# Whole comparisons instead of halves in the routing that runs beside the experts

## The chip, the cores and the metric

The kernel runs on one core of one Trainium2 chip. The metric is the device time of one execution, in microseconds (us); less is better. The engines have short names in the profile: PE is TensorE (matrix products), PEld its weight loads, DVE is VectorE, ACT is ScalarE, POOL is GpSimd, SP is SyncE, which issues DMAs here.

## The reference

Attention over 8 batches, 8 heads, 576 positions of 64 values, in two parts that are added: attention over queries, keys and values averaged in groups of four, repeated four times, and local attention in which each position sees those less than 4 away. The result is seen as 4608 tokens of 512 values. Then a mixture of 8 experts:

```python
logits = x @ w_gate                       # 4608 x 8
order = np.argsort(-logits.flatten())
for idx in order:                         # best pairs (token, expert) first
    tok, e = idx // E, idx % E
    if assigned[tok] >= 0 or counts[e] >= cap: continue   # cap = 4608 / 8 = 576
    assigned[tok] = e; counts[e] += 1
for e in range(E):
    h = np.maximum(x[assigned == e] @ w1[e], 0.0)         # 512 -> 1024
    out[assigned == e] = h @ w2[e]                        # 1024 -> 512
```

Every expert ends with exactly 576 tokens, but which ones follows from a greedy pass over all 36864 logits in order of size.

## The kernel before, in words

**Attention** (the first 290 us) writes the tokens to a table in DRAM and leaves the logits in SBUF: 128 partitions x 36 columns of tokens (`NT` = 36) x 8 experts. Its instructions stand in an order written out by hand.

**Routing** (`Routing`) does not sort. It goes in eight phases, each of which finds the expert that fills up next, the limit in logit value at which it does, and so its list of 576 tokens (`idx`). The best logit of each open token is made an integer key of two 16-bit halves, `xh` and `xl`, each copied 16 wide. To find a limit, `count` compares the key with a set of thresholds, counts per expert how many tokens reach each, and narrows down in three levels: 64 thresholds (`cmp0`, made by `first_compare`), then 32, then 32 (`cmp32`). It is called twice a phase, for the high and the low half. A comparison is a VectorE instruction over (tokens, thresholds) that gives ones and zeros; the counting is a group of TensorE products of these with the marks of each token's best expert (`oh`, `ol`), into a PSUM tile `pR`: 18 products for 64 thresholds, 9 for 32. Small steps follow: `cs`, a product with an identity (line 735), `fl`, a product with ones (line 740), `nj`, and the next thresholds `thr`. Each waits for the one before.

`emit` turns the marks of the chosen tokens into the list. It ranks them, splits the rank into a high and a low part, and makes two one-hot tables, `ohh` (18 wide) and `ohl` (32 wide, line 985); 18 products of `ohl` with `r` (made of `ohh`) give `idx`. The last phase has nothing to search and runs `emit` alone.

Each of these comparisons is cut in parts along the columns of tokens, so that TensorE can start on the first part while VectorE compares the second: `HALF` gives the cuts of `cmp0` and `cmp32` (0 to 20 and 20 to 36), and `EH` those of `ohl` (0 to 18 and 18 to 36).

```python
HALF = {16: ((0, NT),), 32: ((0, 20), (20, NT)), 64: ((0, 20), (20, NT)), 128: ((0, 12), (12, 24), (24, NT))}
EH = ((0, 18), (18, NT))
```

**Experts** (`Experts`): for each, `gather` fetches its rows of the token table into `xg` with GpSimd's indirect DMAs, five pieces (line 1061). ScalarE and VectorE split them into two float16 parts `xs` (lines 1080 and 1081), and DMA transposes issued by SP make `xt` from these. `mlp` multiplies with the first weights into `pH` (line 1097), ScalarE and VectorE make the two parts of `ht` (lines 1110 and 1113), and the second products go into `pX` (line 1126), from where ScalarE and VectorE make `y` (1131 and 1133), which GpSimd scatters to the output (1134). Weights come in as float32 and are split into `wh` (ScalarE, 1044) and `wl` (VectorE, 1046).

**Order.** The first phase runs alone after attention, since the first expert needs its list; the later seven are written ahead of the expert before theirs, with a high priority, so they run beside its products:

```python
for i in range(E):
    if more:
        with tc.high_priority():
            idx2, raw = ro.phase(i + 2 == E, False, ...)
        ...
    ex.mlp(w, xt, idx, in1, in2)
```

From the end of attention on, a planner fixes the order of each engine's instructions before the run, from modelled durations, dependences and priorities. On the chip each engine takes its instructions in that order, and a waiting one holds up those behind it.

Of the kernel before, what the change touches and what calls it, by code (L numbers as in the profile page):

```python
# [30 lines left out]
NT = NTOK // 128  # L31
# [590 lines left out]
CAP = NTOK // E  # L622
LV = ((64, 1024), (32, 32), (32, 1))
SW = 16
HALF = {16: ((0, NT),), 32: ((0, 20), (20, NT)), 64: ((0, 20), (20, NT)), 128: ((0, 12), (12, 24), (24, NT))}
XSB = 2
LOE = "vector"
RACT = True
EH = ((0, 18), (18, NT))
# [15 lines left out]
class Routing:  # L645
# [51 lines left out]
    def compare(self, cmp, key, thr, a, b):  # L697
        w = min(SW, thr.shape[1])
        r = thr.shape[1] // w
        self.nc.vector.tensor_tensor(cmp[:, a:b].rearrange("p t (r j) -> p t r j", r=r),  # L700
                                     key[:, a:b, None, :w].to_broadcast([128, b - a, r, w]),
                                     thr.rearrange("p (r j) -> p r j", r=r)[:, None].to_broadcast([128, b - a, r, w]),
                                     op=OP.is_ge)
# [7 lines left out]
    def count(self, oh, key, cmp, cap):  # L711


        nc, wk = self.nc, self.wk
        base = self.base
        for lv, (J, step) in enumerate(LV):
            if lv:
                cmp = wk.tile([128, NT, J], BF, name=f"cmp{J}")
                for a, b in HALF[J]:
                    self.compare(cmp, key, thr, a, b)  # L720
            n = 128 // J if J < 64 or lv == 0 else 1
            cnt = self.ps.tile([128, 8 * E], F32, name="pR", bufs=2)[:, :n * E]
            cv = cnt.rearrange("p (e i) -> p e i", e=E)
            for t in range(0, NT, n):
                m = min(n, NT - t)
                nc.tensor.matmul(cv[:m * J, :, :m], cmp[:, t:t + m].rearrange("p t j -> p (t j)"), oh[:, :, t:t + m],  # L726
                                 start=t == 0, stop=t + m == NT, skip_group_check=True)
            if n > 1:


                cs = wk.tile([128, 8 * E], F16, name="cs")
                nc.vector.tensor_scalar(cs[:, :n * E], cnt, 2000.0, None, op0=OP.min)
                cnt = self.ps.tile([128, E], F32, name="pR", bufs=2)
                for i in range(n):
                    nc.tensor.matmul(cnt[:J], self.id16[:, J * i:J * i + J], cs[:, i:n * E:n], start=i == 0,
                                     stop=i == n - 1)
            fl = wk.tile([128, E], BF, name="fl")
            nc.vector.tensor_tensor(fl[:J], cnt[:J], cap()[:J], op=OP.is_ge)
            njp = self.ps.tile([128, E], F32, name="pR", bufs=2)
            nc.tensor.matmul(njp, self.one[:J], fl[:J], start=True, stop=True)  # L740
            nj = wk.tile([128, 1], F32, name="nj", bufs=2)
            nc.vector.tensor_reduce(nj, njp, axis=AX.X, op=OP.max)
            if lv < 2:
                w, n = LV[lv + 1][0], base.shape[1]
                thr = wk.tile([128, w], I16, name=f"thr{w}", bufs=2)
                nc.vector.scalar_tensor_tensor(thr, nj.to_broadcast([128, w]), float(step), base[:, :w],
                                               op0=OP.mult, op1=OP.add)
                rest = wk.tile([128, 65], F32, name="rest", bufs=2)[:, :n - w]
                nc.vector.scalar_tensor_tensor(rest, nj.to_broadcast([128, n - w]), float(step), base[:, w:],
                                               op0=OP.mult, op1=OP.add)  # L750
                base = rest
        v = wk.tile([128, 1], F32, name="val", bufs=2)
        nc.vector.tensor_tensor(v, nj, base, op=OP.add)
        return v
# [27 lines left out]
    def setup(self, a, b, first=False):  # L782
# [7 lines left out]
        def t(name, dt=F32, shape=(128, NT), keep=True, mid=False):  # L790
            if not keep:
                return su.tile(list(shape), dt, name=name)[..., a:b]
            if name not in self.v:
                self.v[name] = su.tile(list(shape), dt, name=name)
            return self.v[name][:, a:b] if mid else self.v[name][..., a:b]
# [11 lines left out]
        def spread(x, k):  # L807
            o = t(x, I16, (128, NT, SW), True, True)
            for c in range(0, n, 18):
                d = min(n, c + 18)  # L810
                i = k[:, c:d, None].to_broadcast([128, d - c, SW])
                if first and b < NT and x in SPP:
                    nc.gpsimd.tensor_copy(o[:, c:d], i)
                else:
                    nc.scalar.copy(o[:, c:d], i)
                yield
# [39 lines left out]
    def phase(self, last, first=False, known=None):  # L856
# [4 lines left out]
        def t(name, dt=BF, shape=(128, NT)):  # L861
            return wk.tile(list(shape), dt, name=name)
# [13 lines left out]
        if first:  # L876
            xh = self.v["xh"]
            early = self.first_compare(xh, self.cuts)
# [3 lines left out]
                pass  # L882
        kh, kl, am, amu, oh, xh, xl = [self.v[n] for n in "kh kl am amu oh xh xl".split()]

        if not first:
            early = self.first_compare(xh, HALF[LV[0][0]])
        H = self.count(oh, xh, early, lambda: self.cap)
        cmp0 = self.first_compare(xl, HALF[LV[0][0]])
        e, g = t("e"), t("g")
        nc.vector.tensor_scalar(e, kh, H, None, op0=OP.is_equal)  # L890
        ol = t("ol", BF, (128, E, NT))
# [64 lines left out]
    def emit(self, f, off, first=False, left=None):  # L956


        nc, wk = self.nc, self.wk
        rk = self.rank(f, left)  # L960
        v0, v1 = wk.tile([128, NT], F32, name="v0"), wk.tile([128, NT], F32, name="v1")
        o8 = wk.tile([128, 1], F32, name="o8")
        nc.vector.tensor_scalar(o8, off, -8192.0, None, op0=OP.add)
        nc.vector.scalar_tensor_tensor(v1, rk[:, 1], o8, f[:, 1], op0=OP.add, op1=OP.mult)
        nc.vector.scalar_tensor_tensor(v0, rk[:, 0], -8192.0, f[:, 0], op0=OP.add, op1=OP.mult)
        pi = wk.tile([128, NT], I32, name="pi")
        nc.vector.scalar_tensor_tensor(pi, v0, 8192.0, v1, op0=OP.add, op1=OP.add)
        ph, pl = wk.tile([128, NT], I32, name="ph"), wk.tile([128, NT], I32, name="pl")
        nc.vector.tensor_scalar(ph, pi, 5, None, op0=OP.arith_shift_right)
        nc.vector.tensor_scalar(pl, pi, 31, None, op0=OP.bitwise_and)  # L970
        ph, pl = ph.bitcast(I16)[:, ::2], pl.bitcast(I16)[:, ::2]
        ohh = wk.tile([128, NT, 18], BF, name="ohh")
        nc.vector.tensor_tensor(ohh, ph[:, :, None].to_broadcast([128, NT, 18]),
                                self.io[:, None, :18].to_broadcast([128, NT, 18]), op=OP.is_equal)
        r = wk.tile([128, NT, 2, 18], BF, name="r")
        nc.vector.tensor_tensor(r[:, :, 0], ohh, self.t128, op=OP.mult)
        if first and RACT:
            nc.scalar.activation(r[:, :, 1], ohh, AF.Copy, scale=self.pcol)
        else:
            nc.vector.tensor_scalar(r[:, :, 1], ohh, self.pcol, None, op0=OP.mult)  # L980
        ohl = wk.tile([128, NT, 32], BF, name="ohl")

        p = self.ps.tile([64, 72], F32, name="pR", bufs=2)
        for a, b in EH:
            nc.vector.tensor_tensor(ohl[:, a:b], pl[:, a:b, None].to_broadcast([128, b - a, 32]),
                                    self.io[:, None, :].to_broadcast([128, b - a, 32]), op=OP.is_equal)
            for t in range(a, b, 2):
                nc.tensor.matmul(p, ohl[:, t:t + 2].rearrange("p t i -> p (t i)"),
                                 r[:, t:t + 2].rearrange("p t s i -> p (t s i)"), start=t == 0, stop=t == NT - 2)
        odd = wk.tile([32, 36], F32, name="odd")  # L990
        nc.vector.tensor_copy(odd, p[32:, 36:])
        sm = wk.tile([32, 2, 18], F32, name="sm")
        nc.vector.tensor_tensor(sm.rearrange("p s i -> p (s i)"), p[:32, :36], odd, op=OP.add)
        idx = self.ix.tile([128, 5], I32, name="idx")
        for g in range(4):
            n = (21 - g) // 4
            self.done = nc.vector.tensor_tensor(idx[32 * g:32 * g + 32, :n], sm[:, 0, g::4], sm[:, 1, g::4], op=OP.add)  # L997
        return idx, rk
# [269 lines left out]
```

## Time and profile before

| what | value |
|---|---|
| median of 3 runs | 799.38 us (798.59 to 804.76) |
| the profiled execution | 796.83 us |
| its span, first to last instruction | 795.0 us |
| PE busy | 684.7 us (86%) |
| DVE busy | 562.3 us (71%), 1679 instructions |
| ACT / POOL busy | 333.4 us / 235.1 us |
| attention | 0 to about 294 us |
| first routing, alone | to about 326 us |
| routing beside experts | about 341 to 622 us |
| experts with no routing beside them | about 622 to 795 us |

The page gives busy time per engine, waits with the instruction that ended them, and the clock that TensorE was granted as a share of full speed. In a list in order of time each row has a start, a length, engine, line, operation and shapes; "x9" means that nine like instructions are merged in the row, and a bracket at the end gives the idle time before it and what ended it. Lengths of neighbours may overlap, since the next instruction starts before the last has fully ended; so starts tell the pace, not lengths.

### The profile page before, as it was taken

To read this page: it belongs to the slowest core of one execution; us is meant where nothing else is said; L and a number is where in the kernel's file an instruction comes from. 1 tells how busy PE (TensorE), PEld (TensorE's weight loads), DVE (VectorE), ACT (ScalarE), POOL (GpSimd) and SP (SyncE) were. 2 spreads that over 40 slices of the span, in tenths; PEclk is the share of its full clock that TensorE was granted. 3 is DMA by queue.
4 is the path that set the end of the run, shared out by engine and by line. 5 is a ranking of instruction groups with operands and counts; after the bars stand their busy time and mean duration, and the time that the engine had idled before them with its cause. 6 is when DMAs were issued, how large, how long until landed. Compare 5 with 4: busy or idle time off the path is not lost.

```text
span 795.0 us, 21152 instructions
## 1 busy us (share of the span) xinstructions
PE 684.7 (86%) x8545; PEld 472.8 (59%) x8545; DVE 562.3 (71%) x1679; ACT 333.4 (42%) x631; POOL 235.1 (30%) x274
## 2 busy tenths in 40 slices
PE   6687988796988873499889899999999979999994
PEld 4576877685877752365456356456456456574752
DVE  6878877977797887887869889888869335172210
ACT  3456756573767440342525234234324134252210
POOL 9264463735355440300400412130220311301001
PEclk8789998998999995599989999999999999999997
DMA  9949979697999850611825744480946832704001
GB/s 265 210 129 238 244 195 268 183 255 204 254 228 211 201 173 9 207 66 59 274 60 212 139 151 162 85 307 2 245 147 233 177 113 94 166 1 100 21 28 34
DMA packets 152901, 126.18 MB, mean 159 GB/s; under 512 B 96996, under 2 KB 127204, under 8 KB 152804
## 3 DMA queue, kind: packets, MB, share of 16 engines
q1 hardware_dynamic: 145424, 103.30, 49.9%
q0 software_dynamic: 6432, 20.98, 8.7%
q8 instruction: 68, 1.11, 0.6%
q10 hardware_dynamic: 948, 0.55, 0.3%
q14 instruction: 29, 0.24, 0.1%
HBM read 95.30 MB, written 21.23 MB: 147 GB/s over the span
## 4 chain that ended last, share of the span: by engine, by line
issue 30%; PE 25%; DVE 20%; DMA 13%; ACT 5%; POOL 4%; SPq 2%; POOLq 0%; ACTq 0%; DVEq 0%
PE pH L1097 7%; PE pX L1126 3%; DMA xt<-xs 3%; POOL out_dram L1134 3%; DMA nat<-in_v_dram 2%; DVE cmp L700 2%; PE g L476 2%; PE g L436 2%; PE g L292 2%; DMA xg<-x_dram,idx 2%; PE pR L726 1%; DMA up_dram<-xu 1%; DVE x L407 1%; PE g L454 1%; PE g L325 1%
## 5 line engine op out<-in xcount | busy, mean ns | idle before, releaser
L1097 PE MATMUL pH<-xt,wh 128*128 128x256 f16 (+1 forms) x1024 | 200.1, 291 | 5.7 <-DMA xt<-xs 5.0
L1126 PE MATMUL pX<-wh,ht 128*128 128x512 f16 (+1 forms) x640 | 183.3, 384 | 0.2 <-ACT y L1131 0.2
L1097 PE MATMUL pH<-xt,wl 128*128 128x320 f16 (+1 forms) x512 | 148.5, 290 | 0.0
L1126 PEld LDWEIGHTS <-ht 128*128 128x128 f16 (+1 forms) x960 | 81.5, 101 | 89.2 <-issue 6.4
L1134 POOL DMA_INDIRECT out_dram<-y,idx x40 | 41.2, 1031 | 289.5 <-ACT y L1131 262.9
L1126 PE MATMUL pX<-wl,ht 128*128 128x512 f16 (+1 forms) x320 | 119.3, 384 | 0.0
L1097 PEld LDWEIGHTS <-wh 128*128 128x128 f16 x1024 | 98.2, 99 | 33.2 <-issue 9.1
L1110 ACT ACTIVATE ht<-pH 128x512 f16<-128x512 f32 (+1 forms) x128 | 45.5, 407 | 128.3 <-PE pH L1097 128.3
L1046 DVE SCALAR_TENSOR_TENSOR wl<-nat,wh 128x512 f16<-128x512 f32 x128 | 85.2, 682 | 2.5
L1113 DVE SCALAR_TENSOR_TENSOR ht<-pH,ht 128x512 f16<-128x512 f32 (+1 forms) x128 | 52.4, 450 | 38.7 <-ACT ht L1110 38.3
L1061 POOL DMA_INDIRECT xg<-x_dram,idx x40 | 43.3, 1083 | 118.2 <-DVE idx L997 57.1
L1131 ACT ACTIVATE y<-pX 128x512 f32<-128x512 f32 (+1 forms) x40 | 23.6, 593 | 117.7 <-PE pX L1126 76.4
L1044 ACT ACTIVATE wh<-nat 128x1024 f16<-128x1024 f32 x64 | 66.8, 1055 | 6.6 <-DMA nat<-in_moe_w_dram 6.5
L1081 DVE SCALAR_TENSOR_TENSOR xs<-xg,xs 128x512 f16<-128x512 f32 (+1 forms) x35 | 23.5, 687 | 50.3 <-ACT xs L1080 50.1
L1097 PEld LDWEIGHTS <-wl 128*128 128x128 f16 x512 | 50.6, 99 | 13.0 <-issue 0.4
L465 ACT COPY pt<-g 64x512 f32<-64x512 f32 x72 | 41.8, 580 | 34.2 <-PE g L454 33.0
L292 PE MATMUL g<-ident,nat 128*128 128x128 f32 x256 | 41.7, 292 | 13.7 <-DMA nat<-in_q_dram 9.5
L476 PE MATMUL g<-vw,pt 128*64 128x65 f32 x1152 | 44.5, 230 | 2.4 <-DMA up_dram<-xu 1.4
L476 PEld LDWEIGHTS g<-vw,pt 128*64 128x64 f32 x1152 | 39.5, 143 | 8.4 <-ACT pt L465 4.5
L278 ACT COPY kt<-g 64x512 f32<-64x512 f32 (+1 forms) x56 | 35.1, 627 | 20.7 <-PE g L292 13.8
L278 ACT COPY qz<-g 64x512 f32<-64x512 f32 (+1 forms) x52 | 33.0, 634 | 21.4 <-PE g L292 19.1
L265 POOL TENSOR_TENSOR gtmp<-qz 64x576 f32<-64x576 f32 x28 | 32.5, 1160 | 30.7 <-DVE kdt L268 29.1
(219 smaller groups left out, 1180.1 us busy)
## 6 DMA issues: line engine op xcount, KB each, us to landing
nat<-in_moe_w_dram SPq DMA_DIRECT2D x28, 1024.0 KB
vw<-in_v_dram SPq DMA_DIRECT2D x136, 96.0 KB
up<-up_dram SPq DMA_DIRECT2D x36, 256.0 KB
x_dram<-x SPq DMA_DIRECT2D x36, 256.0 KB
nat<-in_q_dram SPq DMA_DIRECT2D x16, 512.0 KB
nat<-in_k_dram SPq DMA_DIRECT2D x16, 512.0 KB
nat<-in_v_dram SPq DMA_DIRECT2D x14, 512.0 KB
up_dram<-xu SPq DMA_DIRECT2D x16, 128.0 KB
```

The costliest lines, as they stand in the source:

```text
L278: self.nc.scalar.copy(out, in_)
L292: nc.tensor.transpose(p[:, a, :, fp], src[:, 4 * hh + 2 * a + s, 2 * fp:2 * fp + 2].rearrange("p f d -> p (f d)"), self.ident)
L465: self.nc.scalar.copy(out, in_)
L476: nc.tensor.matmul(o[64 * i:64 * i + 64, 65 * h:65 * h + 65], pt[:, 2 * g + i, h].rearrange("p b q -> p (b q)"), self.vw[u % 4][:, i, 4 * ...
L1044: nc.scalar.activation(hi, r, AF.Copy, scale=sc)
L1046: nc.vector.scalar_tensor_tensor(lo[:, a:a + LOP], r[:, a:a + LOP], sc, hi[:, a:a + LOP], op0=OP.mult, op1=OP.subtract)
L1061: self.fetched = nc.gpsimd.indirect_dma_start(out=xg[:n], out_offset=None, in_=self.x, in_offset=bass.IndirectOffsetOnAxis(ap=idx[:n, c:c ...
L1097: mm = nc.tensor.matmul(p[:, s, :s1 - s0], w[d][a][:, 128 * f:128 * f + 128], xt[:, b, d, s0:s1], start=j == 0, stop=j == len(seq) - 1)
L1110: last = nc.scalar.activation(hi, q, AF.Relu)
L1113: nc.vector.scalar_tensor_tensor(lo, q, 0.0, hi, op0=OP.max, op1=OP.subtract)
L1126: nc.tensor.matmul(p[o:o + m], ht[:, f, h0:h0 + m], w[4 + f // 2][b][:, 512 * (f % 2):512 * (f % 2) + 512], start=j < parts, stop=j >= len ...
L1134: i = nc.gpsimd.indirect_dma_start(out=self.out, in_=y[:n], in_offset=None, out_offset=bass.IndirectOffsetOnAxis(ap=idx[:n, c:c + 1], axis=0))
```

## The change

Beside the experts' products each comparison becomes one instruction over all 36 columns, followed by all its products. The first phase (`first`) keeps its cuts. `self.alone` carries that to `count`.

```diff
+WHOLE = ((0, NT),)
...
-                for a, b in HALF[J]:
+                for a, b in HALF[J] if self.alone else WHOLE:
                     self.compare(cmp, key, thr, a, b)
...
+        self.alone = first
+
         if not first:
-            early = self.first_compare(xh, HALF[LV[0][0]])
+            early = self.first_compare(xh, WHOLE)
         H = self.count(oh, xh, early, lambda: self.cap)
-        cmp0 = self.first_compare(xl, HALF[LV[0][0]])
+        cmp0 = self.first_compare(xl, HALF[LV[0][0]] if first else WHOLE)
...
-        for a, b in EH:
+        for a, b in EH if first else WHOLE:
             nc.vector.tensor_tensor(ohl[:, a:b], ...)
             for t in range(a, b, 2):
```

The arithmetic, the products and the DMAs are the same.

## The prediction

> **What bounds the kernel now.** I read the page's busy table first, then the table by stretches of time, then the waits of TensorE inside the stretch that the change touches.
>
> ```profile
> span 795.0 us, 21152 instructions
> ...
> PE 684.7 (86%) x8545; PEld 472.8 (59%) x8545; DVE 562.3 (71%) x1679; ACT 333.4 (42%) x631; POOL 235.1 (30%) x274
> ```
>
> TensorE is busy 86% of the span, VectorE 71%, but the attention, the lone first routing and the experts have different limits, so the average decides nothing. The edit acts only where a routing runs beside the products of an expert, from 341 to 622 us. Columns of the next view: stretch, length, busy us of PE, weight loads, VectorE, ScalarE, GpSimd (instructions), granted clock, DMA share, GB/s.
>
> ```profile
> 341.00:622.00 281.00, 264.63 (x2203) 156.24 (x2202) 237.92 (x836) 103.39 (x191) 51.59 (x47) 0.98 0.50 150
> ...
> 720.50:767.60 47.10, 47.10 (x314) 29.42 (x313) 10.62 (x22) 11.11 (x26) 4.80 (x6) 1.00 0.21 51
> ```
>
> Late in the kernel an expert without routing fills PE completely (47.10 of 47.10). Beside a routing PE still sets the pace, but sits idle 281.00 - 264.63 = 16.4 us, and VectorE is busy 237.92 of 281.00 (85%). So **PE is the bound, with VectorE close behind**; VectorE's time counts where PE waits for it. Three of the largest of these waits:
>
> ```profile
> 393.23 0.24 PE L735 MATMUL pR<-cs,id 128*32 128x8 f16 x4 [1.70 <-DVE cs L732]
> ...
> 405.86 0.63 PE L726 MATMUL pR<-ol,cmp 128*128 128x16 bf16 x18 [2.49 <-DVE ol L892]
> 406.86 0.69 PE L1097 MATMUL pH<-xt,wh 128*128 128x320 f16 x2 [0.37 <-DMA xt<-xs]
> ...
> 453.65 0.16 PE L740 MATMUL pR<-fl,one 32*128 32x8 bf16 x1 [2.31 <-DVE fl L738]
> ```
>
> ```profile
> 391.74 1.33 DVE L1081 SCALAR_TENSOR_TENSOR xs<-xg,xs 128x512 f16<-128x512 f32 x2 [2.05 <-ACT xs L1080]
> 393.00 0.18 DVE L732 TENSOR_SCALAR cs<-pR 128x32 f16<-128x32 f32 x1
> ```
>
> Behind the first of them VectorE was not working: it stood 2.05 us at the `xs` of the gathered rows, with the small routing step `cs` (393.00), for which PE waited, queued behind it in order. A shorter comparison ahead of such a place only lengthens VectorE's own wait there.
>
> **What is removed on VectorE.** Six full routings run beside experts. Each loses one of two instructions at both first comparisons (`cmp0`, keys `xh` and `xl`) and at four comparisons of 32 thresholds; the seventh, short one and these six each lose one at `ohl`: 12 + 24 + 7 = 43 instructions. The elements compared stay. From 325 us to the end, by form (count, busy us, mean ns of one):
>
> ```profile
> L985 DVE TENSOR_TENSOR ohl<-pl,io 128x576 bf16<-128x576 int16 x14 | 10.2, 748 | 0.0
> ...
> L700 DVE TENSOR_TENSOR cmp<-xh,thr 128x640 bf16<-128x640 int16 x12 | 5.8, 484 | 0.0
> L973 DVE TENSOR_TENSOR ohh<-ph,io 128x648 bf16<-128x648 int16 x7 | 5.8, 823 | 0.0
> ...
> L700 DVE TENSOR_TENSOR cmp<-xh,thr 128x512 bf16<-128x512 int16 x12 | 5.0, 416 | 0.0
> L700 DVE TENSOR_TENSOR cmp<-xh,first 128x1280 bf16<-128x1280 int16 x6 | 4.9, 825 | 0.6 <-ACT xh L815 0.4
> ```
>
> Two sizes of the same form give the cost per element, and so an estimate of the whole one: the 32-threshold form (484 - 416)/128 = 0.531 ns, so 1152 elements take 484 + 512 x 0.531 = 756 ns; `cmp0` with the same slope, 2304 elements, 825 + 1024 x 0.531 = 1369 ns; `ohl`, with `ohh` as its second size, (823 - 748)/72 = 1.04 ns, so 1152 take 748 + 576 x 1.04 = 1348 ns. Adding up the two durations would overstate the gain, because neighbours overlap; a pair must be read from start to end in the order of time:
>
> ```profile
> 410.07 0.83 DVE L700 TENSOR_TENSOR cmp<-xl,thr 128x640 bf16<-128x640 int16 x2
> ...
> 427.06 1.43 DVE L700 TENSOR_TENSOR cmp<-xh,first 128x1280 bf16<-128x1280 int16 x2
> ...
> 433.41 1.42 DVE L985 TENSOR_TENSOR ohl<-pl,io 128x576 bf16<-128x576 int16 x2
> ```
>
> The `ohl` pair lasts 1.42 us where its durations sum to 1.50. So a merge saves 1.43 - 1.37 = 0.06 us at `cmp0`, 0.83 - 0.76 = 0.07 at 32 thresholds, 1.42 - 1.35 = 0.07 at `ohl`: 12 x 0.06 + 24 x 0.07 + 7 x 0.07 = **2.9 us of VectorE** over the stretch. How much reaches PE lies between nothing (it is lost at the waits for gathered rows) and all 2.9. The rows of PE that wait for the very operations changed are the nearest:
>
> ```profile
> L988 PE MATMUL pR<-r,ohl 128*64 128x72 bf16 x126 | 6.6, 199 | 4.6 <-DVE ohl L985 3.3 <-DVE r L980 1.3
> L726 PE MATMUL pR<-oh,cmp 128*128 128x32 bf16 x108 | 6.5, 178 | 1.4 <-DVE cmp L700 1.4
> ```
>
> That is 4.6 + 1.4 = 6.0 of the 16.4 us of idle PE; I take the same share, 6.0/16.4 x 2.9 = **-1.1 us**.
>
> **What is removed on PE.** No product goes away; one group takes the place of two. What does a second group cost when its comparison is ready?
>
> ```profile
> 389.63 0.28 PE L726 MATMUL pR<-oh,cmp 128*128 128x32 bf16 x5
> 389.76 0.38 PE L1126 MATMUL pX<-wh,ht 128*128 128x512 f16 x1
> 389.98 0.25 PE L726 MATMUL pR<-oh,cmp 128*128 128x32 bf16 x4
> 390.08 0.38 PE L1126 MATMUL pX<-wh,ht 128*128 128x512 f16 x1
> 390.29 0.38 PE L1126 MATMUL pX<-wl,ht 128*128 128x512 f16 x1
> ```
>
> Read the starts: a product of the expert holds PE for 0.21 us when another follows it (390.08 to 390.29), and 0.22 when a group of counts follows (389.76 to 389.98). So there is no gap, and merging counts saves nothing here; five of them hold PE 0.13 us and four 0.10. At `ohl` there is a gap:
>
> ```profile
> 381.85 0.39 PE L1126 MATMUL pX<-wh,ht 128*128 128x512 f16 x1
> 382.17 0.48 PE L988 MATMUL pR<-r,ohl 128*64 128x72 bf16 x9
> 382.59 0.39 PE L1126 MATMUL pX<-wh,ht 128*128 128x512 f16 x1
> ```
>
> 382.17 - 381.85 - 0.22 = 0.10 us, seven times: **-0.7 us**. The 18 counts on `cmp0` stand in one group already and waited for another operation: the row at 405.86 above (x18) names `ol`, not `cmp`. The early comparison is hidden behind the tokens' marks, so nothing is counted for it on PE; if that cover were gone, PE would wait for its second half, some 0.7 us.
>
> **What is added.** The first group no longer runs under the second comparison. After a 32-threshold comparison nine products follow (0.13 + 0.10) where four did: +0.13 - 0.07 = +0.06 us for whoever needs the count, four times a routing; after `ohl` eighteen follow where nine did, 382.59 - 382.17 = 0.42, less 0.07: +0.35. The routing's chain to its token list grows by 4 x 0.06 + 0.35 = 0.6 us. If every routing were on the path it would be 6 x 0.6 + 0.35 = 4 us; if none, 0. Only the next expert's transposed inputs at 406.86 arrived late (0.37 us), so I count it once: **+0.6 us**. A whole comparison also holds VectorE for up to 1.37 us at a stretch, and the expert's `ht` or the gathered `xs` queued behind it start up to 0.7 us later; that is covered while PE has other products in its queue.
>
> **Where the waits fall** is the unknown term. Each PE order is fixed ahead of time by a planner, and it will be another order after the edit. In the best case the 6.0 us of waits above vanish. In the worst PE arrives at every merged group just as it did at the first half, and waits for the second half too: 24 x 0.416 + 7 x 0.748 = 15.2 us. I take nothing, by the row nearest to the usual case, the gapless group at 389.98.
>
> **Sum:** -1.1 - 0.7 + 0.6 = -1.2 us. The profiled execution took 796.83 us (its span of 795.0 and 1.8 around it) and would take 795.6. The runs' median, 799.38, lies 2.6 us above that execution; with the same step it becomes **798.2 us**.
>
> **The clock, for the rivals' prices.**
>
> ```profile
> 390.00:400.00 10.00, 8.30 (x55) 3.69 (x53) 5.73 (x14) 4.57 (x7) 4.74 (x5) 0.83 0.86 210
> 400.00:420.00 20.00, 16.62 (x149) 10.80 (x148) 14.03 (x50) 3.69 (x9) 1.33 (x1) 0.83 0.16 32
> ...
> 440.00:460.00 20.00, 16.56 (x117) 7.68 (x117) 15.89 (x47) 4.82 (x8) 8.01 (x7) 1.00 0.73 146
> ```
>
> Around the waits of 1.70 and 2.49 us the granted clock fell to 0.83, which lost 0.17 x 10 = 1.7 and 0.17 x 20 = 3.4 us; around the 2.31 us wait it stayed at 1.00. So waits of this size sometimes double their own cost. The Trainium skill, "TensorE: Matmul & The Clock Gate", section "HAM oscillation — how this bites in real kernels", gives the rule that idle gaps of PE should not exceed some 3.4 us; by it no wait here would have cost clock, and the slower rival below would come out 3.4 us lower. The rows at 390 to 420 speak against it as a limit on one gap.
>
> **Rivals.**
>
> *Faster: the new order loses the bad stretch.* If the gathered rows' steps fall elsewhere in VectorE's queue, the waits of 1.70 and 2.49 us go, with the 1.7 + 3.4 us of clock: 9.3 us, so 798.2 - 9.3 = 788.9 us. For it: these waits are accidents of order, not work. Against: they end at transfers that the edit does not touch.
>
> *Slower: PE arrives too early at the merged groups.* PE runs in order, so a group that is not ready stops the expert's products behind it. If PE reaches every merged `ohl` group at the time of today's first half (7 x 0.748 = 5.2 us) and half of the merged counts (12 x 0.416 = 5.0), with one stretch of lower clock (3.4), the sum is +13.6: 811.8 us. It decides from the point where PE reaches most merged groups 0.4 us or more before their comparison ends. For it: `ohl` is already waited for, 3.3 us in all. Against: of the counts only those on `oh` show waits for `cmp`, 1.4 us in 108 products.
>
> *The edit does not do what it says.* Nothing ties the products of one comparison together; the planner may still put an expert's products between them, and the 2.9 us of VectorE may end in its waits: 799.4 us.
>
> **How the numbers follow.** Forecast 0.50, nothing 0.12, faster 0.20, slower 0.18. About 1% (8 us) is what a measurement of this kernel can tell from no change. The first two cases lie inside it, the faster one at -1.3%, the slower at +1.6%: 0.20 faster, 0.62 within, 0.18 slower. The range takes in both rivals' prices, with their farther halves left out: 788 to 812 us.
>
> **What would show it.** The changed profile should have 43 fewer VectorE instructions, whole comparisons near 1.37, 0.76 and 1.35 us, no change before 341 us, and routing groups of 9 and 18 on PE. My step on VectorE is wrong if a pair saved much more than 0.07 us; my zero for the waits is wrong if the idle of PE between 341 us and the last routing differs from 16.4 us by more than 4. The forecast fails most easily by another order of gathers, transposes and weight loads around the experts' borders, which no row here can foretell.

## The result, and the profile after

The changed kernel takes 791.11 us (median of 4 runs, 786.60 to 792.52) where the kernel before, in the same runs, takes 801.38. The ratio is 0.988, with a 95% interval of 0.984 to 0.993: faster by 1.2%. The likeliest time of the prediction was 798.2 us, the range 788 to 812.

The head of the page of the kernel after (its profiled execution took 786.60 us):

```profile
span 784.8 us, 21109 instructions
...
PE 670.7 (85%) x8545; PEld 462.8 (59%) x8545; DVE 559.8 (71%) x1636; ACT 333.4 (42%) x631; POOL 235.6 (30%) x274
```

VectorE runs 43 instructions fewer, as it should, and is busy 2.5 us less. The span is 10.2 us shorter. The whole comparisons, by form (mean ns of one behind the busy us):

```profile
L988 DVE TENSOR_TENSOR ohl<-pl,io 128x1152 bf16<-128x1152 int16 x7 | 9.4, 1350 | 0.0
L701 DVE TENSOR_TENSOR cmp<-xl,thr 128x1152 bf16<-128x1152 int16 x12 | 9.1, 757 | 0.0
L701 DVE TENSOR_TENSOR cmp<-xh,thr 128x1152 bf16<-128x1152 int16 x12 | 9.0, 750 | 0.0
L701 DVE TENSOR_TENSOR cmp<-xh,first 128x2304 bf16<-128x2304 int16 x6 | 8.1, 1354 | 0.5 <-ACT xh L816 0.4
```

They last 1350, 750 to 757 and 1354 ns; the estimates were 1348, 756 and 1369. So the instructions themselves are as expected, and the 10 us must be elsewhere. The table by stretches, first two rows of after, then the second stretch of before and, inside it, the 20 us around a wait that follows below (the last three columns are the granted clock, the DMA share and GB/s):

```profile
341.00:622.00 281.00, 263.33 (x2206) 155.47 (x2207) 233.60 (x792) 101.67 (x186) 53.68 (x49) 0.99 0.50 156
622.00:720.50 98.50, 98.22 (x644) 60.33 (x642) 43.32 (x78) 40.20 (x72) 17.52 (x18) 1.00 0.41 102
```

```profile
622.00:720.50 98.50, 93.74 (x615) 58.60 (x614) 40.65 (x74) 37.15 (x67) 17.61 (x19) 0.98 0.43 104
...
640.00:660.00 20.00, 16.77 (x123) 12.79 (x124) 9.62 (x19) 8.13 (x15) 2.53 (x3) 0.91 0.28 89
```

In the stretch that the edit touches, PE's idle time has not fallen: 281.00 - 263.33 = 17.7 us, 16.4 before. Behind it, where no instruction was edited, before had 4.8 us of idle PE and after 0.3. One wait of before makes nearly all of it, and in after it is missing:

```profile
643.23 0.43 PE L1097 MATMUL pH<-xt,wh 128*128 128x320 f16 x2 [4.60 <-DMA xt<-xs]
```

The transposed inputs of the sixth expert come late. Following the experts by their first store (the POOL scatter of the first output piece) divides the 10.2 us:

| stretch | before, us | after, us | difference |
|---|---|---|---|
| to the first gather of the first expert | 326.24 | 325.56 | -0.7 |
| to the first store of expert 1 | 47.56 | 47.05 | -0.5 |
| experts 1 to 3 | 128.81 | 125.55 | -3.3 |
| experts 3 to 5 | 117.08 | 117.51 | +0.4 |
| **experts 5 to 6** | **53.72** | **47.14** | **-6.6** |
| expert 6 to the last store | 113.14 | 113.53 | +0.4 |

The -6.6 us is the wait of 4.60 us with its lower clock (0.91 over 640 to 660 us, so 0.09 x 20 = 1.8 us). The -3.3 us between experts 1 and 3 goes, in these two traces, with the clock and not with the waits: PE is idle there for 12.3 us in before and 11.7 in after. PE still waits in after:

```profile
391.18 0.39 PE L727 MATMUL pR<-oh,cmp 128*128 128x32 bf16 x9 [2.35 <-DVE cmp L701]
...
397.67 0.39 PE L727 MATMUL pR<-oh,cmp 128*128 128x32 bf16 x9 [1.48 <-DVE cmp L701]
...
404.05 0.55 PE L1100 MATMUL pH<-xt,wh 128*128 128x320 f16 x2 [1.85 <-DMA xt<-xs]
```

```profile
390.00:400.00 10.00, 7.34 (x70) 3.81 (x71) 8.13 (x18) 5.52 (x9) 3.13 (x3) 1.00 0.83 195
400.00:420.00 20.00, 17.79 (x162) 11.88 (x161) 14.06 (x56) 3.27 (x9) 0.91 (x1) 0.91 0.13 25
```

Waits of 2.35, 1.48 and 1.85 us, about as long as before, but the clock lost only 0.09 x 20 = 1.8 us in place of 5.1.

**How the late inputs come about.** A buffer for a 1 MB weight load of the eighth expert becomes free when VectorE makes the last `wl` of the sixth; SP then issues the load (the longest waits of SP's queue before these loads name `wl`). The sixth expert's transposes follow in the same queue, 1.92 us after ScalarE starts on the fifth expert's first output `y`. Rows of three engines, before:

```profile
618.82 0.60 ACT L1131 ACTIVATE y<-pX 128x512 f32<-128x512 f32 x1 [4.98 <-issue]
...
618.97 0.67 DVE L1046 SCALAR_TENSOR_TENSOR wl<-nat,wh 128x512 f16<-128x512 f32 x1
...
619.77 0.37 SPq L1028 DMA_DIRECT2D nat<-in_moe_w_dram  x1
...
620.74 1.66 SPq L1082 DMA_TRANSPOSE xt<-xs  x1
```

and after:

```profile
614.24 0.67 DVE L1049 SCALAR_TENSOR_TENSOR wl<-nat,wh 128x512 f16<-128x512 f32 x1
...
614.79 0.60 ACT L1134 ACTIVATE y<-pX 128x512 f32<-128x512 f32 x1 [4.77 <-issue]
...
615.04 0.37 SPq L1031 DMA_DIRECT2D nat<-in_moe_w_dram  x1
616.72 1.57 SPq L1085 DMA_TRANSPOSE xt<-xs  x1
```

The load stands 0.95 us behind `y` in before and 0.25 us in after: 0.7 us earlier. What that does is in the last two columns (DMA share, GB/s), before and then after:

```profile
626.00:628.00 2.00, 2.00 (x11) 0.88 (x10) 0.00 (x0) 0.00 (x0) 0.00 (x0) 1.00 1.45 218
628.00:630.00 2.00, 2.00 (x11) 0.87 (x9) 0.00 (x0) 0.00 (x0) 0.00 (x0) 1.00 1.04 100
630.00:632.00 2.00, 2.00 (x11) 0.92 (x10) 0.00 (x0) 0.00 (x0) 0.00 (x0) 1.00 0.98 99
```

```profile
620.00:622.00 2.00, 2.00 (x11) 0.92 (x10) 0.00 (x0) 0.57 (x1) 1.00 (x1) 1.00 1.16 306
622.00:624.00 2.00, 2.00 (x11) 0.88 (x9) 0.27 (x1) 0.63 (x1) 0.00 (x0) 1.00 1.16 330
```

In before the DMA engines are full but move 100 GB/s for 4 us; in after the transposes, with gathers and a scatter beside them, go through at 306 to 330 GB/s. The packets of these 4 us, before (628 to 632 us) and then after (620 to 624 us):

```profile
DMA packets 882, 0.40 MB, mean 99 GB/s; under 512 B 835, under 2 KB 835, under 8 KB 882
```

```profile
DMA packets 2336, 1.27 MB, mean 318 GB/s; under 512 B 2153, under 2 KB 2153, under 8 KB 2336
```

The load itself no longer moves in the slow 4 us. By the trace's packet records its last packet ends at 625.2 us in before and at 620.0 us in after, and in both traces the first small packet of the transposes moves just then. So the load stands ahead of the transposes in both. What differs is the time that follows: the small packets of the first two transposes take 7.2 us from the first to the last in before, 3.8 us in after. Why they go so slowly in before is not shown.

VectorE and ScalarE have empty rows there. ScalarE's next piece of gathered rows (`xs`), the third, begins 13.3 us behind `y` in before and 8.3 us in after:

```profile
632.16 0.63 ACT L1080 ACTIVATE xs<-xg 128x512 f16<-128x512 f32 x1 [7.57 <-DMA xg<-x_dram,idx]
```

```profile
623.07 0.63 ACT L1083 ACTIVATE xs<-xg 128x512 f16<-128x512 f32 x1 [2.50 <-DMA xt<-xs]
```

In after the profile names a transpose as what ended the wait. In before it names a gather; but this expert's gathers were issued from 573 to 579 us, so I read that wait too as one for the transposes, since the pieces `xs` have two buffers. That the load's place is the cause, and not a sign of something else, had to be tested.

### The profile page after: what moved, and what is told of

Its sections match the earlier page's. It is cut to its first block, busy times and chain, and to the rows that moved or that the text cites. A ratio compares the mean times of both kernels' runs of the same rounds, so it can differ in the third digit from the quotient of the medians.

```text
span 784.8 us, 21109 instructions
## 1 busy us (share of the span) xinstructions
PE 670.7 (85%) x8545; PEld 462.8 (59%) x8545; DVE 559.8 (71%) x1636; ACT 333.4 (42%) x631; POOL 235.6 (30%) x274
## 4 chain that ended last, share of the span: by engine, by line
issue 30%; PE 25%; DVE 20%; DMA 13%; POOL 4%; ACT 3%; SPq 3%; POOLq 0%; ACTq 0%; DVEq 0%
PE pH L1100 6%; PE pX L1129 5%; POOL out_dram L1137 3%; DMA vw<-in_v_dram 2%; DVE cmp L701 2%; DMA nat<-in_v_dram 2%; PE g L476 2%; PE pR L727 1%; DMA xt<-xs 1%; POOL xg L1064 1%; DVE x L407 1%; DVE xt L499 1%; PE g L436 1%; PE g L292 1%; DMA up_dram<-xu 1%
## 5 line engine op out<-in xcount | busy, mean ns | idle before, releaser
L1100 PE MATMUL pH<-xt,wh 128*128 128x256 f16 (+1 forms) x1024 | 194.7, 288 | 3.6 <-DMA xt<-xs 2.1
L1129 PE MATMUL pX<-wh,ht 128*128 128x512 f16 (+1 forms) x640 | 179.5, 380 | 0.0
L1100 PE MATMUL pH<-xt,wl 128*128 128x320 f16 (+1 forms) x512 | 146.9, 287 | 0.0
```

Source lines behind the costliest of these rows:

```text
L1100: mm = nc.tensor.matmul(p[:, s, :s1 - s0], w[d][a][:, 128 * f:128 * f + 128], xt[:, b, d, s0:s1], start=j == 0, stop=j == len(seq) - 1)
L1129: nc.tensor.matmul(p[o:o + m], ht[:, f, h0:h0 + m], w[4 + f // 2][b][:, 512 * (f % 2):512 * (f % 2) + 512], start=j < parts, stop=j >= len ...
```

## The experiments

All ratios are to the kernel before in the same runs.

**A second trace of before.** No edit.

> The kernel before, unchanged, for a second trace. If the late transposed inputs of the sixth expert (4.60 us of idle TensorE at 643 us, with 1.8 us of lower clock) belong to the order of before, they are there again, between 3 and 6 us. If they were an accident of the one execution, the wait is under 1 us and a third of the 10 us between the two profiled executions is chance. Time: equal to before, ratio 1.00, by either theory; the spread of the runs (798.6 to 804.8 so far) is what it tells.

1.0005 (0.997 to 1.004). The wait is there again, 4.90 us at 646 us, and the stretch from expert 5 to 6 is 55.7 us. It belongs to the kernel, not to one execution. The stretch of experts 1 to 3 is 130.1 us.

**Only the searches whole.**

```diff
-        for a, b in EH if first else WHOLE:
+        for a, b in EH:
```

> Whole comparisons in the searches only (36 of the 43 removed instructions); ohl keeps its halves. If the saved VectorE work is the gain, it scales with it: 36/43 of -10 us, so -8 to -9 us. If the gain is the new order with its two accidents gone, it can be anything between +3 and -10 us, and the trace shows it at the same two places: the clock at 390 to 420 us (3.3 us) and the inputs of the sixth expert at about 640 us (6.2 us).

0.989 (0.984 to 0.994). No wait at the sixth expert, stretch 47.1 us. Both theories allow this.

**Only `ohl` whole.** The searches keep `HALF`.

> Whole ohl only (7 of the 43). If the saved work is the gain: 7/43 of -10 us, so -1 to -2 us, and the wait at 643 us stays. If it is the order: anything between +3 and -10 us, with or without the wait at about 640 us.

1.003 (1.000 to 1.006), with the wait (4.31 us) and a stretch of 55.3 us. The wait stays, as the work theory said, but the 1 to 2 us that it promised lie outside the interval; the theory of order allowed this.

**Other halves, the same work.**

```diff
-WHOLE = ((0, NT),)
+WHOLE = ((0, 18), (18, NT))
+EH2 = ((0, 20), (20, NT))
...
-        for a, b in EH if first else WHOLE:
+        for a, b in EH if first else EH2:
```

> Halves kept beside the experts, only cut elsewhere: the searches at column 18 in place of 20, ohl at 20 in place of 18. The same number of instructions, the same elements, only other halves and so another planned order. If the saved work is the gain: 0 us, within 2. If the order is: it moves too, by 3 to 10 us either way, and where it moves is a wait for transposed inputs or a stretch of lower clock.

0.998 (0.994 to 1.002), the wait 4.30 us. This other order does not move the time; so "it moves too, by 3 to 10 us" is wrong as I had put it. The wait is stable against it.

**Which search.** Only the 32-threshold comparisons, or only `cmp0`, whole.

> Only the 24 comparisons of 32 thresholds whole; cmp0 and ohl keep their halves. If the gain is made by these: -8 us (ratio 0.990) and no wait at 643 us. By saved VectorE work it would be 24 of 43, so -5 to -6 us, with the wait partly there. If the order of cmp0 makes it: 0 us and the wait in full (4.3 to 4.9 us).

> Only the 12 first comparisons whole; the others keep their halves. By saved work 12 of 43, so -2 to -3 us. If the order of cmp0 makes the gain: -8 us and no wait at 643 us; if that of the 32-threshold comparisons does: 0 us and the wait in full.

The 24 comparisons alone give 0.985 (0.982 to 0.989), no wait, 47.1 us; the 12 `cmp0` alone 0.999 (0.996 to 1.003), the wait 4.41 us and 54.1 us. So 24 of the 43 carry all that can be measured. In this kernel too the load is earlier (`y` starts at 620.04 us):

```profile
619.72 0.37 SPq L1031 DMA_DIRECT2D nat<-in_moe_w_dram  x1
621.96 1.47 SPq L1085 DMA_TRANSPOSE xt<-xs  x1
```

**The load out of the way.** The eighth expert's weights behind the sixth expert's last transpose in SP's queue, with halves and with whole comparisons.

```diff
-idx2, raw = ro.phase(i + 2 == E, False, lambda ei: ex.weights(ei, False))
+idx2, raw = ro.phase(i + 2 == E, False, lambda ei: behind(i, ei))
...
+def behind(i, ei):
+    with tc.issue_after(ex.tr[5].ins) if i == E - 2 else nullcontext():
+        return ex.weights(ei, False)
```

> The kernel before with its halves; only the weight loads of the eighth expert are put behind the last transpose of the sixth expert's inputs in SP's queue, so that the 1 MB load issued about 1 us ahead of these transposes no longer runs in front of them. Collision theory (the change gains 6 to 8 us because the load and the scatter no longer fall on these transposes): the wait of 4.3 to 4.9 us at 643 to 648 us and its clock loss go, the stretch from the first store of the fifth expert to that of the sixth falls from 53.7-55.7 to about 47 us, and the time by 6 to 8 us, ratio 0.990 to 0.993. Work theory (the shorter VectorE work brings the inputs sooner): the wait stays, ratio 1.00.

> The same displacement in the kernel after. Collision theory: there is nothing left to gain at that place, the stretch stays at 47 us, and the time equals that of after (ratio 0.986 to 0.991 to before). If the two gains were separate they would add: a ratio of 0.980 to 0.982.

With halves 0.988 (0.984 to 0.991), somewhat more gain than the 0.990 to 0.993 expected; with whole comparisons 0.987 (0.983 to 0.990). SP's rows in the first of them, all five transposes ahead of the loads:

```profile
622.38 13.60 SPq L1084 DMA_TRANSPOSE xt<-xs  x5
637.09 1.01 SPq L1029 DMA_DIRECT2D nat<-in_moe_w_dram  x2
```

The stretch from expert 5 to 6 is 47.0 us and the wait is gone, with all 43 instructions back in place. Once the load is away, whole or half comparisons make no difference that can be measured. One thing is left over: between experts 3 and 5 the profile with halves has 124.3 us, the one with whole comparisons 125.9, where the two traces of before had 117.1 and 120.2. In before the displaced loads stand at 613.34 and 619.77 us, at the end of that stretch, so they can hardly cost it directly; and with no load displaced a kernel had up to 122.2 us there (only `cmp0` whole). Whether the order or chance costs it stays open.

**One instruction, in two places.** The kernel after, where VectorE makes one `wl` twice: the one that frees the buffer (sixth expert), or the same of the seventh.

```diff
-for a in range(0, 1024, LOP):
+for a in range(0, 1024, LOP) if (me, k) != (5, 7) else (0, LOP, LOP):      # or (6, 7)
```

> The kernel after, in which VectorE makes the last 512 columns of the sixth expert's low weights twice, one more instruction of 0.68 us. That instruction frees the buffer into which the 1 MB load goes. Timing theory (the load collides with the sixth expert's transposes when it is issued 0.95 us or more after the fifth expert's first output is taken from PSUM, and does not at 0.25 us or less): the load moves from 0.25 to about 0.9 us, the wait of 4 to 5 us for transposed inputs is back, and the time rises by 6 to 8 us to a ratio of 0.995 to 1.00 to before. Work theory: 0.7 us of VectorE, at most 1 us of time, ratio still 0.987 to 0.990.

> The same one extra instruction, but for the seventh expert's weights, where no load stands ahead of transposes. By both theories within 1 us of after: ratio 0.987 to 0.990, no wait.

With the extra 0.67 us at the sixth expert 794.66 us (0.995, 0.992 to 0.998), at the seventh 787.46 us (0.986, 0.982 to 0.990), side by side on one chip: 7.2 us for one instruction's place. The first of the two, in order of time:

```profile
618.43 0.60 ACT L1136 ACTIVATE y<-pX 128x512 f32<-128x512 f32 x1 [4.77 <-issue]
...
619.17 0.69 DVE L1051 SCALAR_TENSOR_TENSOR wl<-nat,wh 128x512 f16<-128x512 f32 x1
...
620.00 0.37 SPq L1032 DMA_DIRECT2D nat<-in_moe_w_dram  x1
620.55 1.99 SPq L1087 DMA_TRANSPOSE xt<-xs  x1
...
642.83 0.69 PE L1102 MATMUL pH<-xt,wh 128*128 128x320 f16 x2 [4.60 <-DMA xt<-xs]
```

The load now stands 1.57 us behind `y`, and the wait of 4.60 us is back. The load moved further than the 0.9 us expected: in this order VectorE's four `idx` steps, too, come before the `wl` that frees the buffer. In the second the load stays at 0.25 us and no such wait stands. The kernels with two buffers for the gathered pieces, by the place of the load:

| kernel | load behind `y`, us | wait for inputs, us | experts 5 to 6, us |
|---|---|---|---|
| only 32-threshold whole | -0.32 | none | 47.1 |
| searches whole | 0.17 | none | 47.1 |
| after | 0.25 | none | 47.1 |
| after, twice at expert 7 | 0.25 | 0.20 | 47.4 |
| before | 0.95 | 4.60 | 53.7 |
| before, second trace | 0.96 | 4.90 | 55.7 |
| only `cmp0` whole | 0.96 | 4.41 | 54.1 |
| other halves | 1.24 | 4.30 | 53.9 |
| only `ohl` whole | 1.30 | 4.31 | 55.3 |
| after, twice at expert 6 | 1.57 | 4.60 | 53.7 |

Nothing lies between 0.25 and 0.95, and the two groups do not mix. Counted to the sixth expert's first transpose, the split is the same: the load stands 1.67 to 2.24 us ahead of it in the first four rows, 0.55 to 1.09 us in the other six. Which of the two distances counts, these runs do not tell.

**More buffers.**

```diff
-XSB = 2
+XSB = 4
```

> The kernel after with four buffers in place of two for the gathered rows in two parts, so that the third and fourth piece need not wait for the transposes of the first two. If TensorE's waits around 390 to 460 us arise because VectorE and ScalarE stand behind such a piece, they shrink: TensorE's waits between the first stores of experts 1 and 3 fall from 10-11 us to under 7 us, and the time by 3 to 6 us (ratio about 0.983). If those waits come from the planned order alone, they stay at 10 us and the time is that of after.

0.984 (0.979 to 0.988), with 785.38 us the lowest median of the three kernels run side by side, but not told apart from the 0.986 of the extra instruction at the seventh expert. The reason I gave fails: PE's waits between experts 1 and 3 stayed at 10.5 us. So these two buffers are not what holds PE there. The load is early here, 0.83 us ahead of `y`, and a wait of 1.94 us for transposed inputs stands all the same; what the table shows holds for two buffers. With both edits together:

> The kernel after with both: four buffers for the gathered rows in two parts, and the eighth expert's weight loads behind the sixth expert's transposes. In the run with four buffers alone a wait of 1.94 us for transposed inputs stood at 638 us, and the stretch from the fifth to the sixth expert's first store was 50.4 us. Timing theory: with the loads out of the way the wait goes and the stretch is 47 us, so about 3 us less than four buffers alone: a ratio near 0.979. If the wait there comes from the transposes' own later issue (2.44 us after the output is taken, in place of 1.92), it stays at about 2 us and the ratio at 0.983.

0.984 (0.980 to 0.989): the wait of 1.94 us went, 48.3 us from expert 5 to 6, but experts 3 to 5 took 122.4 us again, with the loads displaced. A gain over four buffers alone was not found.

## Why the prediction was right or wrong

**The time and the range.** 791.1 us lies inside 788 to 812, but only because the faster rival's price had widened the range so far. The forecast, a gain of 1.2 us, is far from the 10 us measured, and the rival that came near them named the wrong place. That the range held is luck.

**The bound, PE with VectorE behind it,** holds: PE's idle in the edited stretch changed by 1.3 us, far inside the 4 us that I had set as the limit.

**VectorE's work (-2.9 us, of which -1.1 on PE)** was sized rightly on VectorE: 2.5 us less busy, and the three durations within 20 ns. Reading the pairs from start to end rather than adding durations was the right way. The share of 1.1 us for PE is not shown: PE's idle in the stretch rose.

**PE's groups (-0.7), the longer chain (+0.6) and the waits (0).** The waits on the operations changed, grouped, in after:

```profile
L991 PE MATMUL pR<-r,ohl 128*64 128x72 bf16 x126 | 5.3, 198 | 3.0 <-DVE r L983 1.5 <-DVE ohl L988 1.5
...
L727 PE MATMUL pR<-oh,cmp 128*128 128x32 bf16 x108 | 4.7, 178 | 5.0 <-DVE cmp L701 5.0
```

The products on `ohl` went from 4.6 to 3.0 us of waits and the counts from 1.4 to 5.0, together from 6.0 to 8.0. The count now waits for the whole comparison, as the slower rival said, only far less often than it needed. The sum of these direct terms, -1.2 us, does not contradict the one comparison that isolates them: with the load displaced, whole against half comparisons is 0.987 against 0.988, -0.7 us with some 3 us of uncertainty each way. That they are a gain at all is not shown.

**The step that failed** is the boundary of the sum: "the edit acts only where a routing runs beside the products of an expert, from 341 to 622 us". I counted nothing behind it, though from the first expert's products on PE's largest wait stood at 643 us in the trace of before, 4.60 us for a transfer. That wait's cause lies inside the stretch: a load that VectorE releases at 619.64 us, at the end of the last routing. A shift of 0.7 us there goes with 6.6 us between the two traces, and putting the load behind one instruction more cost 7.2 us. The prediction named gathers, transposes and weight loads around the experts' borders as what could make it fail, and said that no row could foretell it; the row was there, and following it back to the load would have given a rival with the right price, 4.60 + 1.8 us.

**The faster rival** had the size nearly right (788.9 us) and the wrong place: its two waits at 393 and 406 us have successors of the same length. Its clock part came true in the profile, -3.3 us between experts 1 and 3. The other traces show that this is not chance alone: the seven kernels with all searches whole take 125.0 to 127.7 us there, with 9.6 to 11.7 us of idle PE; the five traces with halves in all searches take 128.8 to 131.3 us, with 12.3 to 14.8 us idle. The 24 alone take 129.2, `cmp0` alone 127.2. So beside the wait at the sixth expert the change seems to gain some 4 us here (the means are 125.8 and 130.3), which fits that the kernel with that wait brought back is still 0.5% faster than before. What makes it is not shown, and with the load displaced it does not show in the time.

**The clock rule.** I weighed the limit of some 3.4 us on one gap, from the Trainium skill, "TensorE: Matmul & The Clock Gate", section "HAM oscillation — how this bites in real kernels", against the rows. The one wait of PE above it from the first expert's products on, 4.60 us, stood in a stretch at 0.91 (640 to 660 us), as the rule has it. But none of PE's waits at 390 to 420 us reaches it, and the clock still fell there, to 0.83 in before and 0.91 in after. Which shorter waits cost clock the runs do not settle: in after one of 2.35 us left it at 1.00 (390 to 400 us), and one of 1.85 us stood in the stretch at 0.91.

Why the planner's order puts the last `wl` 0.7 to 1.3 us earlier with whole 32-threshold comparisons is not shown. The saved VectorE time per routing (4 x 0.07 us) is too small for all of it.

## What to carry to other kernels

Before summing up an edit, follow every large wait of the trace back to its cause, also those outside the edited stretch: an edit reaches as far as the buffers that its engines release. A load that waits for a buffer is issued when an engine off the critical path is done; where a short transfer on the path follows it in the same queue, 0.7 us of that engine went with 6.6 us here. An extra instruction at the suspected place and the same one elsewhere is a cheap test of such a cause.

## What the runs showed of the hardware

Where a 1 MB load was issued 0.7 us later, the two transposes behind it, beside gathers and a scatter, took 7.2 us in place of 3.8 (DMA engines full at 100 GB/s in place of 306 to 330, with the load itself already done). In the ten traces with two buffers it looks like a step: at 0.25 us and earlier the wait was at most 0.20 us, at 0.95 to 1.57 us it was 4.3 to 4.9 us each time. Between 0.25 and 0.95 us nothing was measured.
